# Earlier first scores and a column-split last row block in a fused attention and MoE kernel

## The chip, the cores and the metric

The kernel runs on one core of a Trainium2 chip. The metric is the device time of one execution in microseconds (us), where lower is better. Each comparison runs both kernels on the same chip in alternating rounds. A verdict of faster or slower needs 2%, some 8 us here.

Engines: TensorE (PE, with its weight loads as PEld), VectorE (DVE), ScalarE (ACT), GpSimd (POOL) and SyncE (SP). A name with q, such as SPq, is the sequencer of that engine issuing a transfer. A draw is a time that differs between executions of one program.

## The reference

Attention over 8 batches, 8 heads, 576 positions and 64 dimensions per head, with a bias that depends on the distance of two positions, followed by a dense layer with a sine activation. Cut to what matters:

```python
scores = q @ k.T / sqrt(64) + bias_table[bucket(|i - j|)]   # 32 buckets x 8 heads
attn   = softmax(scores);  x = attn @ v                     # x: 4608 tokens x 512
h = x @ w_in                                                # 512 -> 2048
s = sin(alpha * h)
out = (h + s * s / (alpha + 1e-9)) @ w_out                  # 2048 -> 512, float32
```

## The kernel before

The kernel never adds the bias to the scores. It computes exp(scores / 8) on ScalarE and multiplies the diagonal band by exp(bias - last bias row) on VectorE. That factor table is made first: `tabN - tabL`, an exponential, one matmul with a constant `phi_sb`, then a store of 8 KB to DRAM (`e_dram`), from which GpSimd loads the band tables `m2r` and `mhr`. The start, cut (`...` marks cuts):

```python
load_nat(nat0[:, 0], 0, 2, k[0], nc.sync)            # first keys, then queries
load_nat(nat0[:, 1], 0, 2, q[0], nc.sync)
nc.scalar.dma_start(out=tabN, in_=bias_table)
nc.scalar.dma_start(out=tabL, in_=...)               # last bias row, repeated
nc.scalar.dma_start(out=phi_sb, in_=phi_h.ap())
nc.scalar.dma_start(out=alphaN, in_=...)
nc.scalar.dma_start(out=idf_sb, in_=idf.ap())
...
nc.vector.tensor_tensor(out=tabN, in0=tabN, in1=tabL, op=ALU.subtract)
nc.scalar.activation(out=tabE, in_=tabN, func=AF.Exp)
warm(WARM0)
cast0(0, nc.vector)                                  # first keys to f16
cast0(1, P_)                                         # first queries, on GpSimd
turn0(0)                                             # transposes and copy of the keys
nc.tensor.matmul(out=eps_[0:H, 0:EW], lhsT=tabE, rhs=phi_sb, start=True, stop=True)
nc.scalar.activation(out=e_sb, in_=eps_[0:H, 0:EW], func=AF.Copy)
nc.scalar.dma_start(out=e_dram.ap(), in_=e_sb)
turn0(1)                                             # transposes and copy of the queries
load_m2r(P_, 0, 2); load_mhr(P_); cast_v(0, P_, (0, 1)); load_m2r(P_, 2, H) ...
stage_kq(2); load_w_out16(); ...                     # GpSimd, in this order
```

All that follows goes through a planner of the kernel's own. It walks a list of tasks with estimated durations and "not before" times (`T_...`) and emits each engine's instructions in the order that it finds. So the order on TensorE is fixed when the kernel is built. The output of 128 rows is sixteen matmuls of 512 columns, one copy out of PSUM and one store:

```python
def plan_mo(b, a):
    for f in range(NF): ...   full(m.v, gcell[b].v[:, f, 128*a : 128*a+128], w_out16[:, f, :], ...)
    def cp(e):
        o = new_outs()
        copy_on(e, o, m.v)
        nc.sync.dma_start(out=out[r0 : r0 + 128, :], in_=o)
```

The softmax here doesn't subtract the row's maximum and nothing guards it: scores larger than these inputs give would overflow.

Of the kernel before, what the change touches and what calls it, by code (L numbers as in the profile page):

```python
# [20 lines left out]
def t_pe(n):  # L21
    return n / 2400.0 + 0.0025
# [6 lines left out]
def t_dve(n):  # L29
    return n / 960.0 + 0.07  # L30
# [147 lines left out]
D_FLIP = 3.0  # L178
T_MODE = 0.11
T_START = 7.0  # L180
T_FREE = {"PE": 7.0, "ACT": 7.5, "DVE": 7.85}
T_QT0 = 7.85
T_PAIR = ((6.6, 7.3), (10.5, 13.0), (10.5, 13.0))
T_M2 = (16.8, 20.0)
T_MH = (18.0, 18.0)
T_V = (18.5, 50.0)
# [9 lines left out]
CP_PRI = -1  # L196
# [16 lines left out]
def kernel(  # L213
# [211 lines left out]
    def load_nat(dst, h0, h1, src, eng):  # L425

        eng.dma_start(out=dst, in_=src[h0:h1].rearrange("h (p i) d -> p h (i d)", i=SI))
# [13 lines left out]
    def clear(eng, i):  # L441
        eng.memset(kts[i][0:64, :, 64:128], 0.0)
        eng.memset(kts[i][64:128, :, 0:64], 0.0)
        eng.memset(vhs[i][0:64, :, VC : 2 * VC], 0.0)
        eng.memset(vhs[i][64:128, :, 0:VC], 0.0)
        eng.memset(vhs[i][0:64, :, D : D + 1], 1.0)
        eng.memset(vhs[i][64:128, :, VC + D : VC + D + 1], 1.0)
        eng.memset(vs[i][:, :, :, D : D + 1], 1.0)
# [4 lines left out]
    def warm(n):  # L453
        x = bank("moE")
        for _ in range(n):
            full(x, zz[:, 0:128], zz, True, True)

    def cast0(kq, eng):
        eng.tensor_copy(
            out=natb[:, kq], in_=nat0[:, kq].rearrange("s two (i d) -> s i two d", i=SI)  # L460
        )
# [16 lines left out]
    P_ = nc.gpsimd  # L478
    load_nat(nat0[:, 0], 0, 2, k[0], nc.sync)
    load_nat(nat0[:, 1], 0, 2, q[0], nc.sync)  # L480
    nc.scalar.dma_start(out=tabN, in_=bias_table)
    nc.scalar.dma_start(
        out=tabL,
        in_=bass.AP(tensor=bias_table.tensor, offset=bias_table.offset + (NB - 1) * H,
                    ap=[[0, NB], [1, H]]),
    )
    nc.scalar.dma_start(out=phi_sb, in_=phi_h.ap())
    nc.scalar.dma_start(out=alphaN, in_=moe_alpha.rearrange("(f p) -> f p", p=128))
    nc.scalar.dma_start(out=idf_sb, in_=idf.ap())
    nc.scalar.preload_act_table_set(EXP_SET)  # L490
    for kq, src in ((0, k), (1, q)):
        load_nat(nat1[:, kq, 0:2], 2, 4, src[0], P_)
# [13 lines left out]

    nc.vector.memset(zz, 0.0)
    clear(nc.vector, 0)
    nc.vector.tensor_tensor(out=tabN, in0=tabN, in1=tabL, op=ALU.subtract)
    nc.scalar.activation(out=tabE, in_=tabN, func=AF.Exp)  # L510
    warm(WARM0)
    cast0(0, nc.vector)
    cast0(1, P_)

    def turn0(kq):
# [30 lines left out]

    plan = Plan()
    plan.warm = lambda: warm(1)

    def k_of(e):  # L550
        return {"ACT": nc.scalar, "DVE": nc.vector, "POOL": nc.gpsimd}[e]

    def copy_on(e, o, i):
        if e == "ACT":
            nc.scalar.activation(out=o, in_=i, func=AF.Copy)  # L555
        else:
            k_of(e).tensor_copy(out=o, in_=i)  # L557
# [394 lines left out]

    mo_last, cps = [], {}

    def plan_mo(b, a):

        mt = "am" if b < T - 2 else "moL"
        mb, ob, m = Buf(mt), Buf("outs"), Cell()
        for f in range(NF):

            def mm(e, f=f):
                if f == 0:
                    m.v = bank(mb.tag)
                full(
                    m.v, gcell[b].v[:, f, 128 * a : 128 * a + 128], w_out16[:, f, :],
                    f == 0, f == NF - 1,
                )

            mo_last[:] = [plan.add({"PE": t_pe(512)}, mm, mo_last[:] + [gdone[(b, f)]],
                                   500000000 + 4 * b + a, nb=T_WO[f // 4] if b == 0 else 0.0,  # L970
                                   new=[mb] if f == 0 else [],
                                   use=[gbuf[b]] if f == 0 else [gbuf[b], mb])]
            mo_last[0].fill = True

        def cp(e):
            o = new_outs()
            copy_on(e, o, m.v)
            r0 = 512 * b + 128 * a
            nc.sync.dma_start(out=out[r0 : r0 + 128, :], in_=o)

        y = plan.add({"DVE": t_dve(512), "ACT": t_act(512)}, cp, mo_last[:], CP_PRI,
                     new=[ob], use=[mb])
        y.s_only = True
        cps.setdefault(b, []).append(y)
# [10 lines left out]
    for t in range(T):  # L995
        PB = 1000000 * t

        def first(t=t):
            if t == 1:
                load_v16(t + 1)  # L1000
                stage_kq(t + 2)

        def ahead(e, t=t):
            load_kqT(t + 1)
            load_v16(t + 1)
            if t + 2 < T:
                stage_kq(t + 2)

        if 2 <= t < T - 1:
            aheads[t + 1] = plan.add({"SP": 0.1}, ahead, [], PB - 1000000,  # L1010
                                     after=avs[t - 1] + xdone[(t - 1, 1)])
        if t == 1:
            aheads[2] = plan.add({"SP": 0.1}, lambda e: load_kqT(2), list(split_of.values()),
                                 PB - 1000000, nb=T_KQ2)
        if sins:
            gate = [plan.add({"ACT": D_TBL}, lambda e: set_table(EXP_SET), sins, PB)]
        sins = []
        deps, tails = [], []
        for p in range(NP):
            if t == 0 and p + 1 < NP:  # L1020
                for kq in range(2):
                    tr[(0, p + 1, kq)] = plan_tr(0, p + 1, kq, 100 * (16 * p + 8), T_PAIR[p][kq])
            deps.append(pe_gate + (tr[(t, p, 0)][0] + tr[(t, p, 1)][0] if t < 2 else []))
            tails.append(tr[(t, p, 0)][1] if t < 2 else [])
            if (t, p) in split_of:
                tails[-1] = [split_of[(t, p)]]
        early = list(split_of.values()) if t == 1 else []
        if t in aheads:
            early = early + [aheads[t]]
        if t == LAG - 1:  # L1030
            early = early + avs[t - 1] + xdone[(t - 1, 0)] + xdone[(t - 1, 1)]

            def first(old=first):
                old()
                c_mode[0] = 2

        us, ubl, dones, exs = plan_qk(t, deps, tails, first, gate, early)
        exps = exps + exs
        for p in range(NP):
            for w in range(2):  # L1040
                xdone.setdefault((t, w), []).extend(plan_av(t, p, w, us[p], ubl[p], dones[p]))
        if t == 0:
            for p in range(NP):
                for kq in range(2):
                    tr[(1, p, kq)] = plan_tr(1, p, kq, 20000 + 100 * kq + 10 * p, T_TR1[kq])
        if t == LAG - 1:
            continue
        tbl = [plan.add({"ACT": D_TBL}, lambda e: set_table(SIN_SET), exps, PB)]
        bs = [t] if t < LAG else [t - 1] if t < T - 1 else [t - 1, t, t + 1]
        for b in bs:  # L1050
            m, s_ = plan_moe_in(b, tbl)
            sins += s_
        exps = []
        pe_gate = [m]
        for b in bs:
            for a in range(4):
                plan_mo(b, a)
    plan.run(T_START)
    for r in (1, 0, 2):
        regs[r][1].release()  # L1060
# [30 lines left out]
```

## Time and profile before

| | before |
|---|---|
| median of the first three runs | 391.01 us (390.21 to 391.68) |
| span of the profiled execution | 388.9 us |
| first exponential of a score | 10.77 us |
| function-table load to the sine set | 32.51 us |
| last 512-column output copy but one, start | 381.57 us |

The prediction shows most lines of the page that matter. One more is needed below, the clock that TensorE was granted in each fortieth of the span:

```profile
PEclk9999998999999999999999999999999999999999
```

The 8 in the seventh slice is a stretch of 3.4 us at half clock, from 58.2 to 61.6 us by the clock records of the trace. The row hides another stretch: its records begin at 20.6 us, and until then TensorE ran at half clock too, for a matmul of 512 columns took 0.61 to 0.63 us there and 0.38 to 0.39 later.

### The profile page before, as it was taken

The page shows a single profiled execution, that of the slowest core. Times are in us where ns is not written, and L with a number is a line of the kernel's source. Part 1 is how long each engine was busy: PE and PEld are TensorE (multiplying, and loading weights), DVE is VectorE, ACT ScalarE, POOL GpSimd, SP SyncE. Part 2 cuts the span into 40 slices and gives each one's busy share as a digit, 9 for nine tenths or more (in the row PEclk, how much of TensorE's full clock was granted, in tenths as well). Part 3 has the DMA queues.
Part 4 walks back from the last instruction along what each step waited for, and adds up shares of the span by engine and source line. Part 5 has one row for each costly group of instructions (what it writes and reads, how often), then busy time and mean ns, then how long its engine had stood idle before and what let it go on. Part 6 is the DMA issues. An engine that isn't in the chain of part 4 may idle for free.

```text
span 388.9 us, 8502 instructions
## 1 busy us (share of the span) xinstructions
PE 374.5 (96%) x3382; PEld 186.4 (48%) x3382; DVE 264.7 (68%) x587; ACT 319.4 (82%) x450; POOL 82.9 (21%) x98
## 2 busy tenths in 40 slices
PE   5989979999999999999999999999999999999995
PEld 2456435455545544555355535643554444444442
DVE  4686975786886798669767977697669628439100
ACT  2797999999999999999999999999999629539211
POOL 6583935072540081006200400000000000000000
PEclk9999998999999999999999999999999999999999
DMA  9899999999999999939991928210120020020112
GB/s 176 178 203 218 173 191 169 152 159 153 169 143 152 181 126 145 190 59 83 157 159 47 74 33 209 64 27 29 33 68 18 29 81 1 29 81 2 66 68 81
DMA packets 151063, 42.55 MB, mean 109 GB/s; under 512 B 140200, under 2 KB 145408, under 8 KB 151024
## 3 DMA queue, kind: packets, MB, share of 16 engines
q0 software_dynamic: 89872, 19.04, 56.9%
q1 hardware_dynamic: 60928, 22.92, 31.4%
q8 instruction: 26, 0.43, 0.5%
q14 instruction: 13, 0.11, 0.1%
q10 hardware_dynamic: 224, 0.05, 0.1%
HBM read 37.73 MB, written 16.52 MB: 139 GB/s over the span
## 4 chain that ended last, share of the span: by engine, by line
PE 86%; ACT 6%; DVE 3%; issue 2%; DMA 1%; ACTq 0%; DVEq 0%
PE sc L451 40%; PE am L451 37%; ACT u L735 4%; PE ca L451 4%; PE cb L451 4%; ACT s L913 1%; DMA tabL<-in_bias_table_dram 1%; DVE g L927 1%; ACT sq L920 1%; DVE xn L833 1%; DVE u L760 0%; DVE qT L557 0%; PE am L584 0%; PE cb L584 0%; ACT outs L555 0%
## 5 line engine op out<-in xcount | busy, mean ns | idle before, releaser
L735 ACT ACTIVATE u<-sc 128x1024 f16<-128x1024 f32 (+1 forms) x192 | 155.8, 897 | 9.6 <-PE sc L451 8.8
L451 PE MATMUL sc<-xT,w_in 128*128 128x512 f16 x576 | 133.4, 379 | 0.2 <-DVE g L927 0.2
L927 DVE SCALAR_TENSOR_TENSOR g<-sq,inv_a,sc 128x512 f16<-128x512 f16 x144 | 103.8, 746 | 26.0 <-PE am L451 21.4
L451 PE MATMUL am<-w_out,g 128*128 128x512 f16 x448 | 116.8, 381 | 0.7 <-ACT outs L555 0.7
L913 ACT ACTIVATE s<-sc,alphaT 128x512 f16<-128x512 f32 x144 | 92.5, 680 | 6.1 <-PE sc L451 5.5
L760 DVE TENSOR_TENSOR u<-u,m2r 128x512 f16<-128x512 f16 (+2 forms) x160 | 67.6, 439 | 28.4 <-ACT u L735 27.5
L451 PEld LDWEIGHTS <-g 128*128 128x128 f16 x576 | 53.4, 98 | 66.8 <-issue 14.0
L451 PEld LDWEIGHTS <-w_in 128*128 128x128 f16 x576 | 54.5, 98 | 62.8 <-issue 0.5
L451 PEld LDWEIGHTS <-u 128*128 128x128 f16 x1440 | 55.5, 98 | 16.3 <-issue 4.6
L451 PE MATMUL am<-v,u 128*128 128x65 f16 x1216 | 53.0, 194 | 0.0
L451 PE MATMUL sc<-qT,kT 64*128 64x64 f16 (+1 forms) x512 | 48.4, 296 | 4.0 <-ACT u L735 2.4
L920 ACT ACTIVATE sq<-s 128x512 f16<-128x512 f16 x76 | 47.4, 631 | 2.3 <-DVE g L927 0.5
L397 POOL DMA_DIRECT2D v<-in_v_dram x24 | 21.2, 893 | 109.9 <-PE am L451 107.9
L451 PE MATMUL am<-vh,u 128*128 128x130 f16 x152 | 33.6, 222 | 0.5 <-DVE xp L833 0.3
L922 DVE TENSOR_TENSOR sq<-s 128x512 f16<-128x512 f16 x68 | 28.8, 424 | 6.1 <-ACT s L913 5.9
L833 DVE TENSOR_TENSOR xp<-am,rd 128x384 f16<-128x384 f32 (+1 forms) x56 | 27.5, 491 | 2.1
L451 PEld LDWEIGHTS <-kT 64*128 64x128 f16 x512 | 13.8, 95 | 31.3 <-issue 28.3
L832 DVE RECIPROCAL rd<-am 128x6 f32<-128x6 f32 (+1 forms) x60 | 11.3, 188 | 20.2 <-PE am L451 19.9
L555 ACT ACTIVATE outs<-am 128x512 f32<-128x512 f32 x7 | 4.2, 597 | 18.5 <-PE am L451 18.5
L987 ACT ACT_TABLE_LOAD x13 | 16.7, 1283 | 0.2
L557 DVE COPY outs<-am 128x512 f32<-128x512 f32 x21 | 14.4, 687 | 3.5 <-PE am L451 3.3
L378 POOL DMA_DIRECT2D staged_q<-in_q_dram x6 | 14.4, 2395 | 6.8 <-DMA staged_q<-in_q_dram 4.3
(91 smaller groups left out, 169.0 us busy)
## 6 DMA issues: line engine op xcount, KB each, us to landing
out_dram<-outs SPq DMA_DIRECT2D x36, 256.0 KB, 2.0
staged_k<-in_k_dram POOLq DMA_DIRECT2D x6, 576.0 KB, 14.5
staged_q<-in_q_dram POOLq DMA_DIRECT2D x6, 576.0 KB, 19.0
v<-in_v_dram POOLq DMA_DIRECT2D x24, 128.0 KB, 9.1
w_in<-in_moe_w_in_dram POOLq DMA_DIRECT2D x4, 512.0 KB, 7.7
w_out<-in_moe_w_out_dram POOLq DMA_DIRECT2D x4, 512.0 KB, 17.2
xT<-xp SPq DMA_TRANSPOSE x72, 3.8
w_out<-in_v_dram SPq DMA_DIRECT2D x4, 256.0 KB, 9.0
```

What stands on the lines that cost most here:

```text
L378: nc.gpsimd.dma_start(out=dst.ap()[t].rearrange("s (h d) -> s h d", h=H), in_=src[t].rearrange("h s d -> s h d"),)
L397: nc.gpsimd.dma_start(out=vs[t % 2][:, c, :, 0:D], in_=vp[128 * c : 128 * c + 128],)
L451: nc.tensor.matmul(out=out, lhsT=lhsT, rhs=rhs, start=start, stop=stop)
L557: k_of(e).tensor_copy(out=o, in_=i)
L735: nc.scalar.activation(out=o, in_=x, func=AF.Exp, scale=0.125)
L760: nc.vector.tensor_tensor(out=io, in0=io, in1=m2[:, 2 * p : 2 * p + 2, x0 : x0 + hi - lo], op=ALU.mult,)
L833: nc.vector.tensor_tensor(out=y.rearrange("p c (z d) -> p c z d", z=2), in0=a[:, :, :, 0:D], in1=r.unsqueeze(3).to_broadcast([128, nq, 2, ...
L913: nc.scalar.activation(out=s16.v, in_=h.v, func=AF.Sin, scale=alphaT[:, f : f + 1])
L920: nc.scalar.activation(out=sq.v, in_=s16.v, func=AF.Square)
L922: k_of(e).tensor_tensor(out=sq.v, in0=s16.v, in1=s16.v, op=ALU.mult)
L927: nc.vector.scalar_tensor_tensor(out=gcell[b].v[:, f, :], in0=sq.v, scalar=inv_a[:, f : f + 1], in1=h.v, op0=ALU.mult, op1=ALU.add,)
L987: nc.scalar.preload_act_table_set(name)
```

## The change

The intent is that the first keys are cast as soon as they land, that the two small transfers for alpha leave ScalarE's queue, that the first scores no longer wait behind transposes of the next head pair, and that the last copy and the last store move 128 columns instead of 512. The diff, cut:

```diff
-T_FREE = {"PE": 7.0, "ACT": 7.5, "DVE": 7.85}
-T_QT0 = 7.85
-T_PAIR = ((6.6, 7.3), (10.5, 13.0), (10.5, 13.0))
+T_FREE = {"PE": 6.8, "ACT": 7.5, "DVE": 7.75}
+T_KT0 = 6.7
+T_QT0 = 7.75
+T_PAIR = ((6.8, 7.5), (10.0, 12.0), (10.0, 12.0))
...
+    nc.scalar.dma_start(out=phi_sb, in_=phi_h.ap())
     nc.scalar.dma_start(out=tabN, in_=bias_table)
     nc.scalar.dma_start(out=tabL, ...)
-    nc.scalar.dma_start(out=phi_sb, in_=phi_h.ap())
-    nc.scalar.dma_start(out=alphaN, ...)
-    nc.scalar.dma_start(out=idf_sb, in_=idf.ap())
+    nc.sync.dma_start(out=alphaN, ...)
+    nc.sync.dma_start(out=idf_sb, in_=idf.ap())
...
+    cast0(0, nc.vector)
     nc.vector.tensor_tensor(out=tabN, in0=tabN, in1=tabL, op=ALU.subtract)
     ...
-    cast0(0, nc.vector)
...
+    for end in (T_KT0, T_QT0):       # the planner is told when the first two PSUM banks come free
+        x = Task({}, None, [], 0); x.end = end + LAT["DVE"]
+        b = Buf("moE"); b.users.append(x); plan.rings["moE"].append(b)
...
-            for a in range(4):
+            for a in range(3 if b == T else 4):
                 plan_mo(b, a)
+    plan_mo(T, 3, 0, 384)
+    plan_mo(T, 3, 384, DM)
```

`plan_mo` takes a range of columns for this, in its matmuls, its copy and its store, and adds 0.1 us to the planner's estimate of the copy on ScalarE.

More of the change, by code (lines that the diff above doesn't have):

```diff
@@ L486 @@
     )
-    nc.scalar.dma_start(out=phi_sb, in_=phi_h.ap())
-    nc.scalar.dma_start(out=alphaN, in_=moe_alpha.rearrange("(f p) -> f p", p=128))
-    nc.scalar.dma_start(out=idf_sb, in_=idf.ap())
+    nc.sync.dma_start(out=alphaN, in_=moe_alpha.rearrange("(f p) -> f p", p=128))
+    nc.sync.dma_start(out=idf_sb, in_=idf.ap())
     nc.scalar.preload_act_table_set(EXP_SET)
@@ L548 @@
     plan.warm = lambda: warm(1)
+    for end in (T_KT0, T_QT0):
+        x = Task({}, None, [], 0)
+        x.end = end + LAT["DVE"]
+        b = Buf("moE")
+        b.users.append(x)
+        plan.rings["moE"].append(b)
     def k_of(e):
@@ L953, with plan_mo @@
     mo_last, cps = [], {}
-    def plan_mo(b, a):
+    def plan_mo(b, a, c0=0, c1=DM):
         mt = "am" if b < T - 2 else "moL"
@@ L964, in mm @@
                 full(
-                    m.v, gcell[b].v[:, f, 128 * a : 128 * a + 128], w_out16[:, f, :],
-                    f == 0, f == NF - 1,
+                    m.v[:, 0 : c1 - c0], gcell[b].v[:, f, 128 * a : 128 * a + 128],
+                    w_out16[:, f, c0:c1], f == 0, f == NF - 1,
                 )
-            mo_last[:] = [plan.add({"PE": t_pe(512)}, mm, mo_last[:] + [gdone[(b, f)]],
+            mo_last[:] = [plan.add({"PE": t_pe(c1 - c0)}, mm, mo_last[:] + [gdone[(b, f)]],
                                    500000000 + 4 * b + a, nb=T_WO[f // 4] if b == 0 else 0.0,
@@ L976, in cp @@
             o = new_outs()
-            copy_on(e, o, m.v)
+            copy_on(e, o[:, 0 : c1 - c0], m.v[:, 0 : c1 - c0])
             r0 = 512 * b + 128 * a
-            nc.sync.dma_start(out=out[r0 : r0 + 128, :], in_=o)
-        y = plan.add({"DVE": t_dve(512), "ACT": t_act(512)}, cp, mo_last[:], CP_PRI,
+            nc.sync.dma_start(out=out[r0 : r0 + 128, c0:c1], in_=o[:, 0 : c1 - c0])
+        y = plan.add({"DVE": t_dve(c1 - c0), "ACT": t_act(c1 - c0) + 0.1}, cp, mo_last[:], CP_PRI,
                      new=[ob], use=[mb])
```

## The prediction

> **What bounds the kernel now.** I read the slice rows of the page first, then the chain of work that ended last, then the timeline of the two ends, because the change touches only the ends.
>
> ```profile
> PE   5989979999999999999999999999999999999995
> ACT  2797999999999999999999999999999629539211
> PE 86%; ACT 6%; DVE 3%; issue 2%; DMA 1%; ACTq 0%; DVEq 0%
> ```
>
> One digit is a fortieth of the 388.9 us span, 9.7 us. From the seventh slice on TensorE is at 9 to the end; PE is 86% of the chain. The waits of PE between 60 and 200 us sum to 0.2 us and between 200 and 372 us to 1.0 us, so nothing can be gained there, but a head start that TensorE has at 66 us should reach the end whole. The two soft places are the first 58 us and the last slice. The chain in order of time over the first 48 us says what the first softmax waits for:
>
> ```profile
> 1.26 4.10 DMA tabL<-in_bias_table_dram
> 5.46 0.71 DVE tabN L509
> 6.17 0.66 DVE natx L459
> 6.88 0.66 PE cb L518 x6
> 7.54 0.51 PE am L528
> 8.06 0.61 PE am L518 x6
> 8.69 0.77 DVE qT L521
> 9.50 0.69 PE am L584 x12
> 10.19 0.56 PE sc L451 x2
> 10.77 1.03 ACT u L735
> ...
> 16.90 4.48 ACT u L735 x5
> ```
>
> A 1 KB bias row (tabL) lands at 5.36 us; VectorE, which runs in order, subtracts it and only then casts the first keys, which have been in SBUF since 4.3 us (issued at 0.81, landing 3.5 us later). The first query copy ends at 9.45. Then TensorE does twelve transposes of the second head pair before the first score matmuls, and the first exponential starts at 10.77. The end is:
>
> ```profile
> 381.32 3.62 PE L451 MATMUL cb<-w_out,g 128*128 128x512 f16 x16
> 385.03 0.60 ACT L555 ACTIVATE outs<-cb 128x512 f32<-128x512 f32 x1 [2.86 <-PE cb L451]
> 385.65 0.33 SPq L979 DMA_DIRECT2D out_dram<-outs  x1
> ```
>
> Sixteen matmuls, one copy of 0.60 us and a 256 KB store stand in a row; nothing else runs. By the packet records of the trace, the store's data moves from about 386.75 to 387.5 (128 packets of 2,048 bytes at 86 ns, eight per DMA engine).
>
> **What the Trainium skill says.** (1) "SBUF — State Buffer", Who interferes with whom: a VectorE instruction with two SBUF inputs and a GpSimd instruction that reads SBUF exclude each other, for the whole instruction. The trace agrees:
>
> ```profile
> 5.34 0.82 POOL L459 CAST natx<-natx 96x768 f16<-96x768 f32 x1 [0.65 <-DMA natx<-in_q_dram]
> 5.46 0.71 DVE L509 TENSOR_TENSOR tabN<-tabN,tabL 32x8 f32<-32x8 f32 x1 [2.69 <-DMA tabL<-in_bias_table_dram]
> ```
>
> A 32x8 subtraction shows 0.71 us and ends at 6.17, when GpSimd's cast ends (6.16). (2) "DMA: Bandwidth & Descriptors", Anatomy of one DMA: a fixed cost of about 2.0 us, mostly the write receipt. The page's row of output stores has 2.0 us to landing, data included, so only the data part can shrink. (3) "TensorE: Matmul & The Clock Gate", LDWEIGHTS: a weight load takes its columns over 1.2 per ns, 107 ns for 128. If that were the rate, 128-column matmuls would be bound by weights. The trace differs: 27 matmuls of 65 to 130 columns with 128-column weights take 1.01 us of the chain, 37 ns each. (4) Same page, Part 1: the clock falls to half after an idle window of some 3.4 us, on windows that run free. The trace has such a stretch: granted clock 0.72 in 57 to 63 us.
>
> **The change part by part.** The instruction orders of the two builds, with buffer names left out, differ on TensorE only in the first 540 or so of 6,800 rows and in the last row block; on ScalarE only in the DMA issues ahead of the first exponential and in the last copy. So the sum has two terms.
>
> *Start.* VectorE now casts the keys as soon as they land: 4.35 to 5.07 (0.72 us). The keys' transposes (0.66) are done near 5.8. The subtraction follows the cast; tabL is now third on ScalarE's queue behind the 32 KB phi and tabN, issued at about 1.72. The third of that queue before, phi, landed at 7.1 (1.74 plus 5.4), but behind a value load of 1,024 descriptors of 256 bytes that SyncE issued at 1.75; now alpha and its identity (16 descriptors each) stand there and the values come about 0.9 us later. Between the second place (5.36) and 7.1 I choose 5.9. The subtraction then still waits for GpSimd's cast, to 6.2, and ends about 6.35. From there the old durations: exponential of the table to 6.6; phi matmul 6.65, 0.52 until the next group starts; query transposes 7.17; the query copy 0.70 after their start, 7.87, done 8.63 against 9.45. Gain 0.8.
>
> The known banks make the scheduler put the first scores straight after that copy instead of behind twelve more transposes: scores at 8.7 against 10.12, first exponential 0.65 later, 9.35 against 10.77. Gain 1.4. In the new order each score group is separated by one transpose group (0.69 at the half-speed of this stretch) and 0.6 of scores, against exponentials of 0.97, so ScalarE is nearly kept fed: my walk along the new order, with the durations above, puts the first exponential of the second pair at 15.4 against 16.90, gain 1.5. After that the band product matters: the new order does two score groups of pair three before the weighted sum of pair one, and VectorE is nearly full (4.4 of 5 us busy in 30 to 35). I get 0.6 of idle ScalarE twice, where before there were two gaps of 0.3. That leaves 1.0 to 1.2 at the last exponential (32.5 before).
>
> *What can take it back.* The weights w_out land from a queue that is full from 19 us on. The waits of the issuing engine show their landings:
>
> ```profile
> 62.19 2.20 POOL L378 DMA_DIRECT2D staged_k<-in_k_dram  x1 [3.04 <-DMA w_out<-in_moe_w_out_dram]
> 63.32 1.24 PE L451 MATMUL am<-w_out,g 128*128 128x512 f16 x5
> 65.29 2.20 POOL L378 DMA_DIRECT2D staged_q<-in_q_dram  x1 [0.90 <-DMA w_out<-in_moe_w_out_dram]
> 66.18 0.38 PE L451 MATMUL am<-w_out,g 128*128 128x512 f16 x1
> ```
>
> The fourth piece lands at 65.3 and is first used at 66.2: 0.9 us of margin. A start that is over 0.9 earlier is cut to that there, unless the loads come earlier too. They may: the table's store waits for the phi matmul, which comes 0.8 earlier, and GpSimd's later issues hang on that store. But the store issued at 8.71 moved its packets only at 12.0, behind the values, so I count half. I take 1.0 for the start.
>
> *End.* The last 128 rows become 384 and 128 columns. Matmuls: 3.45 us for 16 of 512 is 216 ns each; 16 of 384 take 2.6, 16 of 128 about 56 ns each, 0.9; the sum is 0.05 more. The last copy goes to VectorE: 687 ns for 512 columns, less 384 columns at 0.96 per ns, 0.29 instead of 0.60: gain 0.31. The store of the 384 columns is issued under the last matmuls. The last store has 128 packets of 512 bytes at 40 ns (the alpha load's packets), eight per engine, 0.33 instead of 0.69: gain 0.36. Together 0.65 with the 0.05 taken off, rounded.
>
> Sum: 1.0 + 0.65 = 1.65; 391.0 less 1.65 is **389.4 us**.
>
> **Rivals.** *A, tabL is late.* It lands at 7 as phi did; the key copy waits behind the subtraction on VectorE, the phi matmul starts at 7.5 as before, and the query copy gains nothing. Only the new order is left, 0.6 at the first exponential. With the end: 389.9 to 390.2. For it: small loads of this queue took 2.8, 4.1 and 5.4 us in order of place. Against it: the value load behind which phi stood is now later. *B, the start is absorbed.* ScalarE's gain is lost to VectorE and the band tables by 33 us, or to w_out at 66. Then only the end counts: 390.3. For it: the 0.9 margin and VectorE's load; against it, the margins of the other three pieces are 1.3 us and more, and the keys and queries of the second batch land at 35.8 and 39.7 for uses at 38.9 and 45.2. *C, the whole head start arrives*, loads included, and the gaps in ScalarE's row close: 1.8 plus 0.65, 388.5. *D, the clock.* The stretch of half clock at 57 to 63 costs about 1 us; with all stages shifted it may vanish or double. It has no preferred sign and widens the range.
>
> **Range and chances.** I give my own account 45%, A 20%, B 15%, C 20%. Their values run from 388.5 to 390.3; the three runs of before differ by 1.5 us, and D adds about as much. So 8 in 10: 388.1 to 390.7. Faster by over 2% would need 383.2, five times the whole gain; slower by over 2% needs a broken overlap that the equal orders after row 540 speak against.
>
> **What would show it.** In the profile after: the key cast near 4.4; the subtraction ending near 6.4; query copy near 7.9; first exponential at 9.0 to 9.7; the last exponential before the table load ending 1.0 to 1.2 earlier than 32.5; the first w_out matmul of the fourth piece waiting little or not; the last output copy near 0.29 us and the span ending about 0.65 sooner after the last 512-column group than before. Wrong if the subtraction waits for tabL beyond 7, if exponentials start later than 10, if PE shows a new wait on a w_out, w_in or band load, or if the last 128-column matmuls take over 100 ns each.

## The result

In five runs each the changed kernel takes 389.34 us in the median (389.07 to 390.38) and the kernel before 390.73 us (390.17 to 391.68). The ratio is 0.9967, with a 95% interval of 0.9946 to 0.9989. A ratio is the mean time of one kernel's runs over that of the other's of the same rounds, so it is not quite the ratio of the medians that are quoted. Executions over 1.5% slower than the fastest of the same kernel are left out of the means. The profiled executions have spans of 388.9 us before and 387.7 us after.

The page after shows the same picture as before for TensorE and ScalarE, and a chain whose shares differ in one point, 3% of transfers and 2% of GpSimd:

```profile
PE   6989979999999999999999999999999999999996
ACT  2996999999999999999999999999999728539210
PE 86%; ACT 5%; DMA 3%; DVE 2%; issue 2%; POOL 2%; ACTq 0%; DVEq 0%
```

The chain of waits after, in order of time (start, duration, what), tells what that is:

```profile
1.71 4.57 DMA tabL<-in_bias_table_dram
...
8.07 5.41 DMA e_dram<-e_sb
13.77 0.73 POOL m2r L466
...
21.24 1.06 PE am L452 x27
...
23.27 2.49 ACT u L742 x3
```

The chain no longer runs through ScalarE's first exponentials. It runs through the store of the factor table, which takes 5.41 us to land, then through GpSimd's band loads and value casts, to the first weighted sum of values at 21.24. That is one execution: in after_again, the same program, the chain ahead of the first weighted sum runs through TensorE's own order instead, with one exponential in it.

The timeline after at the start (start, duration, engine, line, operation, idle time before and what ended it):

```profile
4.59 0.56 DVE L460 CAST natx<-natx 96x768 f16<-96x768 f32 x1 [1.81 <-DMA natx<-in_k_dram]
...
5.52 0.82 POOL L460 CAST natx<-natx 96x768 f16<-96x768 f32 x1 [0.84 <-DMA natx<-in_q_dram]
...
6.39 0.15 DVE L511 TENSOR_TENSOR tabN<-tabN,tabL 32x8 f32<-32x8 f32 x1 [1.24 <-DMA tabL<-in_bias_table_dram]
```

The keys are cast at 4.59 instead of 6.10. The subtraction itself takes 0.15 us once GpSimd's cast is over. The query copy starts at 8.05 (8.69 before) and the first exponential at 9.51 (10.77 before).

The end after:

```profile
380.78 2.76 PE L452 MATMUL cb<-w_out,g 128*128 128x384 f16 x16
...
383.38 1.06 PE L452 MATMUL am<-w_out,g 128*128 128x128 f16 x16
383.64 0.56 DVE L564 COPY outs<-cb 128x384 f32<-128x384 f32 x1 [23.18 <-PE cb L452]
384.53 0.29 DVE L564 COPY outs<-am 128x128 f32<-128x128 f32 x1 [0.34 <-PE am L452]
```

The 384-column copy lies beside the last matmuls, and the last copy takes 0.29 us.

The first reload of ScalarE's function table comes after the last exponential of the first batch. Before and after:

```profile
32.51 1.28 ACT L987 ACT_TABLE_LOAD   x1
...
31.82 1.28 ACT L994 ACT_TABLE_LOAD   x1
```

**Where the time went.** Three reloads of ScalarE's function table, at about 32, 54 and 96 us, and the last full 512-column output copy that both kernels have (381.57 before, 381.03 after) cut the span into pieces that can be compared across kernels. All numbers are read from the timelines, in us. "Half clock" is the time at half clock between 55 and 63 us.

| profile of | first reload | to second | to third | to last full copy | from it to the end | span | half clock |
|---|---|---|---|---|---|---|---|
| before | 32.51 | 22.14 | 41.22 | 285.70 | 7.37 | 388.94 | 3.4 |
| before_again | 31.95 | 22.12 | 41.17 | 285.68 | 7.37 | 388.29 | 3.4 |
| end_only | 31.79 | 22.11 | 41.95 | 285.70 | 6.63 | 388.17 | 6.8 |
| start_only | 31.39 | 22.41 | 40.66 | 285.71 | 7.37 | 387.54 | 0 |
| arrive_only | 31.80 | 22.52 | 41.03 | 285.70 | 6.63 | 387.68 | 3.4 |
| plan_only | 31.43 | 22.11 | 41.47 | 285.70 | 6.63 | 387.34 | 3.4 |
| after | 31.82 | 22.43 | 41.11 | 285.68 | 6.62 | 387.65 | 3.4 |
| after_again | 31.63 | 22.65 | 41.14 | 285.70 | 6.62 | 387.76 | 3.4 |
| store_early | 31.68 | 22.28 | 41.09 | 285.70 | 6.62 | 387.37 | 3.4 |
| band_sync | 31.71 | 22.42 | 41.02 | 285.70 | 6.38 | 387.23 | 3.4 |
| alpha_act | 32.01 | 22.22 | 42.16 | 285.70 | 6.63 | 388.72 | 3.4 |
| av_late | 32.19 | 22.19 | 42.27 | 285.71 | 6.63 | 388.99 | 6.8 |
| store_av_late | 31.72 | 22.19 | 42.26 | 285.70 | 6.63 | 388.50 | 6.8 |
| av_late_alpha | 31.88 | 22.41 | 40.88 | 285.70 | 6.63 | 387.49 | 0 |

From the third reload to the last full copy all fourteen profiles agree within 0.03 us over 286 us. So everything that happens ahead of 96 us, losses included, reaches the end whole. The end is a constant of the build, except that band_sync ended 0.25 sooner, which lies behind the landing of its last store: 0.99 us from there to the end of the span, against 1.22 in after. Between the means of the two profiles of each kernel (before and before_again, after and after_again) the first reload is 0.50 earlier, the stretch to the second is 0.41 longer, the next 0.07 shorter and the end 0.75 shorter, which makes the 0.91 between the mean spans. **The end gave its gain; the start gave most of its own back before 54 us.** The draws of the two starts overlap: end_only, with the old start, has its first reload at 31.79, inside the 31.39 to 31.82 of the changed start (start_only, after, after_again).

**Where the start lost it.** The first batch has 24 exponentials ahead of the first reload, six for each pair of heads. Their start times, as means of the same two profiles of each kernel:

| | before | after | gain |
|---|---|---|---|
| first exponential | 10.53 | 9.41 | 1.12 |
| first of the second pair | 16.65 | 15.15 | 1.50 |
| first of the third pair | 21.58 | 20.61 | 0.97 |
| first of the fourth pair | 26.90 | 26.14 | 0.77 |
| first reload | 32.23 | 31.73 | 0.50 |

The first 0.53 is lost in the second pair, all of it ahead of the first weighted sums of after and after_again (21.24 and 21.04). From the first exponential to the reload it takes 21.63 to 21.84 us in the four profiles with the planner's old constants (before, before_again, end_only, arrive_only) and 22.00 to 22.33 in the seven with its new ones and T_V as it was, whatever the order of transfers. So it is the new order of instructions that uses the head start up. TensorE in the second pair, in after and in start_only (zz is a tile of zeros; the planner puts such a matmul where it expects TensorE to idle, and it reckons with full clock from the start):

```profile
15.70 0.61 PE L452 MATMUL sc<-qT,kT 64*128 64x512 f16 x2
16.24 0.61 PE L452 MATMUL am<-zz 128*128 128x512 f16 x1
16.78 0.61 PE L452 MATMUL sc<-qT,kT 64*128 64x512 f16 x2
17.32 0.61 PE L452 MATMUL cb<-zz 128*128 128x512 f16 x1
...
17.23 0.39 PE L452 MATMUL cb<-zz 128*128 128x512 f16 x1
17.60 0.39 PE L452 MATMUL sc<-qT,kT 64*128 64x512 f16 x2
```

At half clock a group of scores and a matmul on zeros come every 1.08 us, while exponentials of 1,024 columns that wait for nothing follow each other every 0.90. In after two of them start 1.08 us after the one before; in start_only, where TensorE was at full clock by then, the same two keep to 0.90 to 0.92. The change to full clock is a draw: the clock records have it at 16.8 us in start_only, 19.4 in after, 20.1 in after_again and 20.9 in end_only. With the new constants the second pair took 4.97 us where it came at 16.8, 5.30 at 19.0 (plan_only, band_sync), 5.40 at 19.4 and 5.53 at 20.1. Why the change comes so late is not shown: in before TensorE was busy 94% of the 13.65 us ahead of it. No run left the matmuls on zeros out, so their part is not shown either.

### The profile page after: what moved, and what is told of

It reads as the page before. It is cut to its first block, busy times and chain, and to the rows that moved or that the text cites. A ratio compares the mean times of both kernels' runs of the same rounds, so it can differ in the third digit from the quotient of the medians.

```text
span 387.7 us, 8540 instructions
## 1 busy us (share of the span) xinstructions
PE 374.2 (97%) x3398; PEld 186.9 (48%) x3398; DVE 265.0 (68%) x589; ACT 319.2 (82%) x449; POOL 82.5 (21%) x98
## 4 chain that ended last, share of the span: by engine, by line
PE 86%; ACT 5%; DMA 3%; DVE 2%; issue 2%; POOL 2%; ACTq 0%; DVEq 0%
PE sc L452 40%; PE am L452 38%; PE ca L452 4%; PE cb L452 3%; ACT u L742 2%; DMA e_dram<-e_sb 1%; ACT s L920 1%; DMA tabL<-in_bias_table_dram 1%; DVE g L934 1%; ACT sq L927 1%; POOL v L418 1%; DVE qT L564 0%; POOL mhr L473 0%; POOL m2r L466 0%; POOL vh L421 0%
## 5 line engine op out<-in xcount | busy, mean ns | idle before, releaser
L452 PE MATMUL am<-w_out,g 128*128 128x512 f16 (+1 forms) x464 | 118.2, 376 | 0.7 <-ACT outs L562 0.7
L452 PEld LDWEIGHTS <-g 128*128 128x128 f16 x592 | 54.5, 98 | 66.3 <-issue 14.0
L398 POOL DMA_DIRECT2D v<-in_v_dram x24 | 21.2, 893 | 105.0 <-PE am L452 103.0
L564 DVE COPY outs<-am 128x512 f32<-128x512 f32 (+1 forms) x22 | 14.7, 669 | 3.9 <-PE am L452 3.4
```

The costliest lines, as they stand in the source:

```text
L398: nc.gpsimd.dma_start(out=vs[t % 2][:, c, :, 0:D], in_=vp[128 * c : 128 * c + 128],)
L452: nc.tensor.matmul(out=out, lhsT=lhsT, rhs=rhs, start=start, stop=stop)
L564: k_of(e).tensor_copy(out=o, in_=i)
```

## The experiments

Twelve runs were made, two of them of the unchanged kernels. All of them gave correct results.

**end_only**: the kernel before, with the last block split.

```diff
-def plan_mo(b, a):
+def plan_mo(b, a, c0=0, c1=DM):       # and the two calls of the last block, as in the change
```

> The old start with the new end (last 128 rows as 384 and 128 columns). My theory: the two ends add up. The profiles of before and after differ in the end by 0.70 us (from the copy of the last full 512 columns that both have, at 381.57 and 381.03, to the end of the span: 7.37 and 6.67), so this kernel should be 0.7 us under before (0.998) with the first exponential at 10.8 as before. Rival: the end is worth less because the store of the 384 columns stands in the way of the last one, and the start made up the rest: 0.3 us or less.

Measured: 390.2 us, ratio 0.9975 (0.9955 to 0.9995). In the profile the end is 6.63 instead of 7.37, a gain of 0.74. Its span of 388.17 hides that, because this execution had two half-clock stretches and its stretch from the second to the third reload is 0.8 longer than with one.

**start_only**: the changed kernel with the last block whole (`plan_mo` too is as before, not shown), so the new start alone.

```diff
-            for a in range(3 if b == T else 4):
+            for a in range(4):
                 plan_mo(b, a)
-    plan_mo(T, 3, 0, 384)
-    plan_mo(T, 3, 384, DM)
```

> The new start with the old end. My theory: the start is worth 0.54 us (copy of the last full 512 columns at 381.03 against 381.57), so 0.5 us under before, 0.9986; the first exponential at 9.5 as after. Rival: the head start of 1.26 at the first exponential would be worth more than 1 us, and the profiled run of after only fell in a bad phase of the clock: then 1 us or more under before.

Measured: 390.22 us, ratio 0.9978 (0.9961 to 0.9996). The end is back at 7.37. The short span of 387.54 comes with an execution without a half-clock stretch (40.66 in the third column of the table). The two timings cannot rank the halves: each interval is about as wide as the effect.

**arrive_only**: new order of transfers and key cast first, with the planner's old constants; new end.

```diff
-T_FREE = {"PE": 6.8, "ACT": 7.5, "DVE": 7.75}
-T_KT0 = 6.7
-T_QT0 = 7.75
-T_PAIR = ((6.8, 7.5), (10.0, 12.0), (10.0, 12.0))
+T_FREE = {"PE": 7.0, "ACT": 7.5, "DVE": 7.85}
+T_QT0 = 7.85
+T_PAIR = ((6.6, 7.3), (10.5, 13.0), (10.5, 13.0))
```

The loop that enters the known banks is taken out as well.

> Of the start, only the DMA order and the key cast ahead of the subtraction; the scheduler's constants and first banks are those of before, the end is the new one. First exponential at about 10.1 (scores stand behind twelve more transposes). Theory 1, the values' casts on GpSimd, which start when the table's store has landed (13.5 to 13.7 in both), set the first weighted sum: it starts at 21.2 to 21.5 all the same, and the time is within 0.2 us of after. Theory 2, the order of TensorE is what made the start's gain: the time is about 0.5 us over after.

Measured: 389.41 us, ratio 0.9964 (0.9947 to 0.9981). The query copy starts at 8.08 and the first exponential at 10.16. The first weighted sum came at 21.04, a little ahead of the 21.2 to 21.5 of theory 1, and the time is that of after, against theory 2.

**plan_only**: the planner's new constants and known banks, with the old order of transfers and casts; new end.

```diff
-    nc.scalar.dma_start(out=phi_sb, in_=phi_h.ap())      # back behind tabL
-    nc.sync.dma_start(out=alphaN, ...)                    # back on ScalarE
-    nc.sync.dma_start(out=idf_sb, in_=idf.ap())           # back on ScalarE
-    cast0(0, nc.vector)                                   # back behind the exponential
```

> Of the start, only the scheduler's constants and first banks; DMA order and cast order as before, the end is the new one. First exponential near 10.15 (query copy still done at 9.45, then scores at once). Theory 1 (GpSimd's chain sets the first weighted sum): it starts at 21.0 to 21.4, and the time is within 0.2 us of after. Theory 2 (earlier data made the gain): about 0.5 us over after.

Measured: 389.47 us, ratio 0.9959 (0.9944 to 0.9974). The first exponential starts at 9.41, not at 10.15 as expected, and the first reload comes at 31.43. Part of that is a draw: the old order had its subtraction at 4.91 here and its query copy at 7.95, not at 8.69. What the planner's part does by itself is the time from the query copy to the first exponential, 1.46 us here and in after, and 2.08 or 2.09 in the four profiles with the old constants: 0.62. The new order of transfers adds little that these profiles show: the query copy starts at 7.86 to 8.69 in the four profiles with the old order, and at 7.84 to 8.08 in after, after_again, start_only and arrive_only. The stretch of plan_only to the second reload is 22.11, not the 22.4 to 22.7 of the changed kernel. It lost time later: TensorE waited 0.31 us for the fourth piece of w_out at 65.33.

**before_again**: the kernel before, unchanged, to see what the comparison can resolve.

> The kernel before, unchanged, with a profile of its own. In the first profile of before GpSimd's cast of the queries (from 5.34) held the bias subtraction for 0.71 us; in the profiles of end_only and plan_only, which have the same start, the subtraction began first and took 0.15. Theory: this is a race that one execution wins and another loses, so the first exponential of before is at 9.9 or at 10.8 from run to run, and the profile that I predicted from had lost it. Then this profile shows one of these two values. Rival: those kernels differ from before in some way that I overlooked, and before always shows 10.8. The time against before: ratio 1.000, and its interval is the noise floor of all these comparisons (some 0.2%).

Measured: 390.12 us, ratio 0.9988 (0.9963 to 1.0013). Two identical kernels differed by 0.1% here, and the interval is 0.5% wide, more than the whole effect. Its profile shows something else. The profile that I predicted from had an unlucky start:

```profile
5.19 0.15 DVE L509 TENSOR_TENSOR tabN<-tabN,tabL 32x8 f32<-32x8 f32 x1 [2.42 <-DMA tabL<-in_bias_table_dram]
5.35 1.15 POOL L459 CAST natx<-natx 96x768 f16<-96x768 f32 x1 [0.69 <-DMA natx<-in_q_dram]
```

In this execution VectorE's subtraction began 0.16 before GpSimd's cast and took 0.15 us. In the first profile it began 0.12 after the cast and was held for 0.71, as the prediction's first point from the skill has it. The same program has its first exponential at 10.28 here and at 10.77 there. That is neither of the two values that I expected, because here TensorE waited for phi, which landed at 6.94 (7.14 in the first profile, 6.51 in end_only): the old order has two such draws. Two of the other kernels with the old order of transfers (end_only, plan_only) also got 0.15.

**after_again**: the changed kernel, unchanged.

> The changed kernel, unchanged, for more executions and a second profile. Expected: 0.9965 of before, first exponential 9.4 to 9.5, the table's store landing at 13.3 to 13.8 and the first weighted sum 7.4 to 7.5 us after that (20.8 to 21.2). If the first weighted sum does not follow the store's landing, the theory of GpSimd's chain falls.

Measured: 389.77 us, ratio 0.9969 (0.9944 to 0.9994), as in the first comparison. The subtraction ran at 6.14 and the first exponential at 9.30. GpSimd's first band load, which waits for the store, came at 13.62 and the first weighted sum 7.42 later, at 21.04, as expected; yet the chain of this execution does not run through the store, so that the two times fit is no proof. The stretch to the second reload is 22.65, longer still than after's, because a square on VectorE was held by GpSimd's value casts.

**store_early**: the table's store is issued by SyncE between its second and third value load, to take it from behind the queued values.

```diff
-    for c in range(4):
+    for c in range(2):
         nc.sync.dma_start(out=vst[0][:, c], ...)
...
-    nc.scalar.dma_start(out=e_dram.ap(), in_=e_sb)
+    nc.sync.dma_start(out=e_dram.ap(), in_=e_sb)
+    for c in range(2, 4):
+        nc.sync.dma_start(out=vst[0][:, c], ...)        # and the two small value loads behind these
```

> After, with the store of the exponentials' table issued by SyncE between the second and the third value load, so that no more than half of the values can stand ahead of it. Theory: the store lands near 11 instead of 13.5, GpSimd's chain starts that much earlier, but the last values land 1 to 2 us later and their casts close the chain; first weighted sum at 19.5 to 20.5, time 0.3 to 0.8 us under after. Rival: the store's landing is bound by its own latency (5 us), not by the values ahead of it: then it lands at 13 as before and nothing is gained.

Measured: 388.83 us, ratio 0.9951 (0.993 to 0.9971). GpSimd's first band load starts at 12.80 instead of 13.62 to 13.77, so the store did land 0.8 to 1.0 earlier. Yet the timeline has the first weighted sum at 21.08, against 21.24 in after and 21.04 in after_again. By the chain of waits of store_early, what leads to it is TensorE's own order and the exponentials:

```profile
18.52 2.20 ACT u L744 x3
...
20.76 0.39 PE sc L452 x2
21.15 1.00 PE am L452 x27
```

The score matmuls wait for a buffer that ScalarE empties, and the weighted sum stands behind them on TensorE.

**band_sync**: the three band loads are issued by SyncE, to take them out of GpSimd's program.

```diff
-    load_m2r(P_, 0, 2)
-    load_mhr(P_)
+    load_m2r(nc.sync, 0, 2)
+    load_mhr(nc.sync)
...
-    load_m2r(P_, 2, H)
+    load_m2r(nc.sync, 2, H)
```

> After, with the three band loads issued by SyncE instead of GpSimd, so that GpSimd casts the values without waiting for the table's store, and its cast of the last values ends near 17 instead of 21. Theory (GpSimd's chain sets the first weighted sum): the first weighted sum starts at 19.5 to 20.3, after the band products on VectorE, and the time is 0.5 to 1.0 us under after. Rival (TensorE's order and the exponentials set it): the weighted sum stays at 20.7 or later and the time at that of after.

Measured: 389.1 us in the median, four fast runs of 388.76 to 389.25 and two slow ones of 398.28 and 400.5; ratio of the fast runs 0.995 (0.9926 to 0.9975). GpSimd's last value cast started at 17.74 instead of 20 and later, and the first weighted sum still came at 21.12. So the chain through the store, the band loads and the value casts is one of several that end near 21 us. Taking it away alone did not move the weighted sum, and the theory that it alone absorbs the head start has fallen. As GpSimd is 2 to 3 us ahead here, its weight loads are too: the fourth w_out piece was there 3 us before its use.

**alpha_act**: the changed kernel with alpha and its identity loaded by ScalarE again. The changed kernel has a stop on ScalarE that no wait explains, 12 us after the first reload:

```profile
44.13 0.69 ACT L920 ACTIVATE s<-sc,alphaT 128x512 f16<-128x512 f32 x1 [0.34 <-ACT s L920]
```

ScalarE had no other work, and the releaser named is its own previous instruction. Counted from the reload this sine starts at 12.29 or 12.30 in after, after_again, arrive_only, start_only and band_sync, and at 11.99 or 12.00 in before, before_again, end_only and plan_only. What those four share is the old order of transfers, with two more transfers in ScalarE's program.

```diff
-    nc.sync.dma_start(out=alphaN, ...)
-    nc.sync.dma_start(out=idf_sb, in_=idf.ap())
+    nc.scalar.dma_start(out=alphaN, ...)
+    nc.scalar.dma_start(out=idf_sb, in_=idf.ap())
```

> The changed kernel with one thing undone: alpha and the identity matrix are again loaded by ScalarE, after the last bias row, instead of by SyncE. Theory (ScalarE stops for 0.3 us at a fixed place of its own instruction stream, 12 us after the second table load, because its stream is two DMA issues shorter): the stop of 0.32 to 0.34 us at that Sin is gone, second table load to first score of t=1 goes from 21.34 to 21.57 back to 21.0 to 21.1, first exponential stays at 9.3 to 9.5, ratio about 0.9958. Rival (the stop comes of the order of data or of TensorE, not of ScalarE's stream): it stays at 0.3 us, ratio as the changed kernel's, 0.997.

Measured: 389.23 us, ratio 0.9967 (0.995 to 0.9983). The stop is gone: three sines follow each other without a gap, and the one in question is at 11.99.

```profile
42.69 2.00 ACT L920 ACTIVATE s<-sc,alphaT 128x512 f16<-128x512 f32 x3
```

The stretch to the second reload fell to 22.22. So moving these two transfers to SyncE does cost 0.3 us there. But the time did not fall: in the profile, which is of the slowest of the six executions, TensorE waited at 66 us for weights (below), and the two half losses that I had added up as independent were not.

**av_late**: one constant of the planner, so that TensorE does four more scores before the first weighted sum.

```diff
-T_V = (18.5, 50.0)
+T_V = (21.0, 50.0)
```

> The changed kernel with one constant of its planner raised, the time at which the first values may be used (18.5 to 21.0 us): TensorE's fixed order then holds four more 512-column scores ahead of the first weighted sum. Theory (TensorE's order, weighted sums ahead of the next scores, is what leaves ScalarE idle for 0.67 us at 23.3 us): that gap falls to under 0.3, the second table load comes at 31.2 to 31.4 instead of 31.63 to 31.82, ratio 0.9955 to 0.9965. Rival (the late value casts set it, or the gap only moves on): first weighted sum later, ScalarE's idle time the same in sum, table load at 31.6 to 31.8 or later, ratio 0.997.

Measured: 389.49 us, ratio 0.9976 (0.9959 to 0.9994). The gap only moved, as the rival said:

```profile
24.78 1.14 ACT L742 ACTIVATE u<-sc 128x576 f16<-128x576 f32 x2 [0.72 <-PE sc L452]
...
28.80 1.02 ACT L742 ACTIVATE u<-sc 128x1024 f16<-128x1024 f32 x1 [0.46 <-PE sc L452]
```

The first exponential came early at 9.00, and the first reload was the second latest at 32.19. Neither is what T_V was to show. By its clock records TensorE ran at full clock from 4.5 to 7.9 us in this execution, and at half clock from there to 18.1. And the planner answered the constant with more than the scores: it put two copies on ScalarE ahead of the reload that VectorE makes in after.

```profile
26.02 0.49 ACT L562 ACTIVATE xT<-am 128x384 f16<-128x384 f16 x1
...
29.72 0.48 ACT L562 ACTIVATE xT<-am 128x384 f16<-128x384 f16 x1
```

The three runs with T_V at 21.0 all have them, 0.97 us together, so their first reloads do not compare with the others', and what the later weighted sum does by itself is not shown. Their times do compare: none has a lower ratio than the 0.9967 and 0.9969 of the changed kernel. The profile of av_late is of the slowest of its six executions.

**store_av_late**: both edits, the early store and T_V at 21.0.

> The same constant raised, together with the table's store issued by SyncE between the second and the third value load, as in the run store_early. Theory (with the store early the values are ready by 20.5 us, and TensorE's order is the last thing in the way): table load at 31.1 to 31.4, no stop at a Sin that reaches the end, ratio 0.994 to 0.995 (store_early alone had 0.9951). Rival (the gaps before the table load are absorbed by the half-speed TensorE anyway): as store_early, table load 31.6 to 31.7.

Measured: 389.89 us, ratio 0.9986 (0.9971 to 1.0001), first reload at 31.72, near what the rival expected (store_early: 31.68), though with the two copies ahead of it and with the first exponential at 8.79, the earliest of all, after another early stretch at full clock (4.0 to 7.4).

**av_late_alpha**: T_V at 21.0 and alpha on ScalarE.

> The constant raised and alpha and the identity matrix loaded by ScalarE again: both suspected losses of the start taken away at once, the table's store left where the changed kernel has it. If both theories hold, their gains add: 0.3 us (no stop at the Sin) and 0.3 us (table load at 31.2 to 31.4), ratio about 0.995, span 386.9 to 387.2. If only the stop goes, ratio about 0.996; if neither, 0.997.

Measured: 389.92 us, ratio 0.999 (0.9973 to 1.0008), first reload at 31.88. The theory that the two gains add has fallen. In the profile the sine has no 0.3 stop, but the stretch is 22.41 all the same, because ScalarE waited 0.24 us for scores at 48.19. The span of 387.49 is short because this execution had no half-clock stretch.

**The weights at 66 us.** GpSimd's wait for the fourth w_out piece and TensorE's first use of it stand close together. After:

```profile
65.85 2.20 POOL L379 DMA_DIRECT2D staged_q<-in_q_dram  x1 [0.90 <-DMA w_out<-in_moe_w_out_dram]
65.59 0.38 PE L452 MATMUL am<-w_out,g 128*128 128x512 f16 x1
```

And alpha_act:

```profile
66.91 2.20 POOL L379 DMA_DIRECT2D staged_q<-in_q_dram  x1 [0.98 <-DMA w_out<-in_moe_w_out_dram]
66.65 0.38 PE L452 MATMUL am<-w_out,g 128*128 128x512 f16 x1 [0.84 <-DMA w_out<-in_moe_w_out_dram]
```

Where TensorE does wait for this piece (alpha_act, plan_only) it starts 0.26 us before GpSimd's next instruction, which waits for the same piece. Taking 0.26 off GpSimd's time in after gives a landing at 65.59, the very time of TensorE's matmul: no margin was left in that execution. By the same count the landing was at 65.03 in before, 64.82 in before_again, 64.47 in after_again and 61.93 in band_sync, for uses near 65.4 to 66.2. The landing does not follow the head start. It follows GpSimd by some 21 us: the issue of the last piece came at 44.0 in before, 43.6 and 44.4 in the changed kernel's two profiles, 40.8 in band_sync and 45.7 in alpha_act, after its own waits for w_in and the second batch.

## Why the prediction was right or wrong

The predicted time of 389.4 us stands beside a measured 389.34. The sum is less right than it looks: its start was oversized, its end a little undersized, and that the sum came out at the measured median is luck: the profiles give 0.91 for the 1.65 of the sum, and the median of before that it starts from was itself a draw (391.01 in the first three runs, 390.73 in five).

**The end, 0.65: right, measured 0.74 to 0.75.** The copy gained 0.31 as predicted (0.60 to 0.29). The matmuls cost 0.04: from the start of the last full copy to that of the last copy it takes 3.50 us after and 3.46 before. The mis-sized term is the store, put at 0.36 and measured at 0.48: from its issue to the end of the span it took 3.29 us before (385.65 to 388.94) and 2.81 after (384.85 to 387.66), of which 2.00 and 1.58 are to its landing. The prediction took 40 ns for a 512-byte packet from another load; the packets of this store took 27 ns, and all 128 started within 0.32 us, against 0.74 for the 2,048-byte ones (from 386.5 on, 0.3 earlier than the prediction reads; no sum rests on it).

**The start, 1.0: oversized.** Each of its steps, against after and after_again:

- The key cast at 4.35 came at 4.59, and took 0.56. Nearly right.
- "The second place (5.36) and 7.1 I choose 5.9" for tabL: it landed at 6.0 to 6.3, a little later than chosen, and the subtraction ended at 6.54 and 6.34 (predicted 6.35).
- Query copy 7.87 (8.05 and 7.84) and first exponential 9.35 (9.51 and 9.30): right.
- "First exponential ... 9.35 against 10.77. Gain 1.4": the number after was right and the number before was one draw. The subtraction of before races GpSimd's cast for the shared port, and it lost in the profile that I read. In before_again it won, and the first exponential came at 10.28. Half a microsecond of the predicted gain was that draw. I had shown the two lines and read them as a fixed cost of the old order. The same holds for "Gain 0.8" at the query copy: over four profiles of each order of transfers the means of its start are 8.17 and 7.98, 0.2 apart. The planner's part, which rival A puts at 0.6, measured 0.62.
- "15.4 against 16.90, gain 1.5": right, 15.25 and 15.04, and 1.50 between the means.
- "I get 0.6 of idle ScalarE twice" and "That leaves 1.0 to 1.2 at the last exponential (32.5 before)": this is the step that failed. Of the 1.50 at the second pair 0.50 was left at the first reload, not 1.0 to 1.2; against the profile predicted from alone it moved by 0.69 and 0.88. The long gap was there (0.67 and 0.58 at 23 us). Two other losses were not in the walk. One lies in the second pair, 0.53 between the means: the walk took ScalarE as nearly kept fed, but TensorE at half clock, with the planner's matmuls on zeros between the scores, fed it too slowly. The other is 0.27 in the fourth pair, with a new gap of 0.15 at 31.2. Store_early and band_sync show that the late store and GpSimd's band loads alone do not hold the start back (first reload at 31.68 and 31.71). That the new order does it is shown by the profiles of the old and the new constants; how much of it is half clock and how much the matmuls on zeros stays open.
- What the prediction did not have at all is the loss of 0.3 us by a stop of ScalarE at 44 us, which the move of alpha to SyncE brings. Alpha_act shows that putting the two transfers back takes the stop away. Why it is there is open. It came only in the five profiles where ScalarE has 63 entries in the trace ahead of this sine, and not with 61, 62, 64, 65 or 66 (av_late and store_av_late have no stop although SyncE loads alpha there: 64 and 62 entries). That points at a place in the program and not at data, but no run tells what happens at that place. The instruction packets in the trace don't tell either: after has one at 36.4 and the next at 48.5.

**The rivals.** A (tabL as late as 7) did not happen. B (start absorbed) was the nearest: 0.17 of the start is left at the last full copy, on which the means of before and after are at 381.25 and 381.08. It named the right places, the stretch to 33 us and w_out at 66 us, but for the first a cause, VectorE and the band tables, that band_sync does not bear out. The 0.9 us of margin that I read for w_out's fourth piece (1.15 by the count above) was again one draw: it is nil in after, and negative in plan_only and alpha_act, whose waits of 0.31 and 0.84 went straight into the span. C (whole head start) did not happen. D (the clock) was right in kind. With one stretch of 3.4 us the piece from the second to the third reload takes 41.0 to 41.2 where no weights are waited for, with none 40.66 and 40.88, with two 41.95 to 42.27. One stretch more or less is worth as much as the whole start, so single profiles cannot be compared by their spans. The idle window of the prediction's fourth point from the skill is not in these traces: in the 3.4 us before its clock fell, before's TensorE was busy 45% of the time, end_only's 56%, and after 58% in start_only and 61% in av_late_alpha at that place (counted in steps of 3.41 us from the clock's first change) no stretch came.

**Total.** The timings of after and after_again, 0.9967 and 0.9969, are worth 1.2 to 1.3 us of 391. The profile pairs give 0.91, of which the end is 0.75. Sorted by clock, the timings agree with the profiles. Of the executions with a mean granted clock of 0.995 or 0.996, which is what one half-clock stretch of 3.4 us gives, before and before_again have 19 with a mean span of 388.6, and the changed kernel six with 387.75, which is 0.9 less. Start_only has two of them (388.4 and 388.6) and end_only two (387.2 and 387.5): few, but they say too that the end is most of it.

**Versions that may beat the changed kernel.** Store_early had six runs of 388.65 to 389.67 us beside 388.68 to 390.33 for after_again in the same rounds, and a span 0.39 shorter. Their means are 0.7 us apart, but the two ratios, 0.9951 and 0.9969, have overlapping intervals. At a granted clock of 0.995 or 0.996 store_early has spans of 387.1, 387.1 and 387.4, and after_again of the same rounds 387.6, 387.8 and 388.4. Band_sync looks equal (387.0 to 387.5) but showed slow runs. Neither is settled.

## What to carry to other kernels

A head start is worth what the order behind it leaves, so follow it through several later points (here 1.12, 1.50, 0.97, 0.77 and 0.50 us) and not only to the first. A planner that reckons with full clock does not know a stretch at half clock: look how long a matmul takes there. A race between engines for a port or a transfer's landing is a draw, and a margin read from one execution is one sample of it: profile the old kernel twice before pricing what removes it. A shorter tail that nothing overlaps (last copy, last store) can be priced from the trace to a tenth of a microsecond, and arrives.

## What the Trainium skill lacked or had wrong

- No page has it: ScalarE stopped for 0.30 us at one sine with all its inputs ready, and the stop went away when two transfers were put back into its program (12.30 to 11.99 us after the reload).
- "DMA: Bandwidth & Descriptors", Anatomy of one DMA, gives some 2.0 us as the fixed part and lets the rest scale with bytes, for transfers that GpSimd issues. The last stores, which SyncE issues, took 2.0 us to landing for 256 KB and 1.6 for 64 KB: the difference is near what the page's rate gives (an estimate of 0.45 us), but what is left as the fixed part is some 1.4 us and not 2.0. At the start a store of 8 KB took 5.41 us and the last bias row of 1 KB 4.57 us. The page has no figure from which that can be worked out.
- "TensorE: Matmul & The Clock Gate", Back-to-back issue gap, gives 131 ns per matmul of 512 columns and 81 ns per matmul of 128 as sustained rates with their weight loads. Here 16 of 512 columns took 3.45 us, 216 ns each, which is the page's figure for a matmul by itself, and 16 of 128 columns 1.06 us with the tail included, 66 ns each.
